# Two MLP products by seven block products each, beside each other, in an attention and MLP kernel

## The chip, the cores and the metric

The kernel runs on one core of one Trainium2 chip. The core has TensorE (PE in the profile; its weight loads are PEld), VectorE (DVE), ScalarE (ACT), GpSimd (POOL) and SyncE (SP), which work at the same time and wait for each other through semaphores; each takes its own instructions in order. 16 DMA engines move data between HBM and the on-chip memory SBUF. TensorE writes its results to PSUM, which has eight banks of 128 partitions x 512 fp32 numbers. The metric is the time of one execution in microseconds, the median of several runs; lower is better.

## The reference, cut to what matters

There are 4 sequences of 768 positions and 8 heads of width 64. Attention with decay, block by block (the reference uses blocks of 64; the kernel uses blocks of 128, which gives the same sums):

```python
intra = np.einsum('bhic,bhjc->bhij', qb, kb) * Dmask[None]      # lam ** (i - j) for i >= j
intra = np.einsum('bhij,bhjd->bhid', intra, vb)
inter = np.einsum('bhid,bhde->bhie', qb * lam_pow[None], kv_state)
out[:, :, sl] = intra + inter
kv_state = lam_block * kv_state + np.einsum('bhsd,bhse->bhde', kb * rev_pow, vb)
...
x = attn_out.transpose(0, 2, 1, 3).reshape(B * S, H * D)         # 3072 x 512
h = x @ w_in                                                     # 512 x 2048
g = 0.5 * h * (1.0 + erf(h / sqrt(2)))
return g @ w_out                                                 # 2048 x 512
```

## The kernel before

The 24 chunks (4 sequences of 6 chunks of 128 positions) are taken in order of the sequence: chunk n belongs to sequence n // 6. Four chunks in a row form a group of 512 rows; there are six groups. The MLP of group g and the attention of group g+1 are issued together, so that TensorE alternates between them.

The MLP of a group is a list of blocks (`mlp_blocks`, line 276). The first product has 16 blocks (`mm1`, line 281): four matmuls of 128 x 128 x 512 into one PSUM bank, then ScalarE's Gelu writes 512 columns of g in bf16 (line 290). The second product goes by 128 rows (`mm2`, line 295): 16 matmuls of 512 columns into a bank in four parts, then ScalarE copies the bank to SBUF (line 305) and SP stores it (line 306). The last 128 rows of the last group go in two halves of 256 columns (`mm2_half`, line 309, matmuls on line 315).

The attention of a chunk has these steps. POOL issues the loads of k, q and v (`load`, line 63), which turn fp32 into bf16 and read rows of 64 numbers. Each load waits until the POOL load eight places before it has landed. For the first two groups k and q are transposed by TensorE (line 174), from chunk 8 on by DMA from SP's queue (`dma_transposes`, line 185), after POOL has multiplied q by its decay (line 190). POOL multiplies k by its decay too (line 167). `scores` (line 193) makes eight small matmuls and DVE masks them (line 202). `next_state_full` (line 234) makes four matmuls, and DVE adds the old state (line 245) and multiplies by the decay (line 246). `outputs` (line 249) makes four matmuls with the state and eight with v, and ACT or DVE copies the result to the x of the MLP.

The order for TensorE is written out by hand for groups 0 and 1 (lines 371 to 397 and `group0`, line 425), and from chunk 8 on it is by due times, as shares of a group's work (`todo`, line 438). In the first microseconds TensorE also runs matmuls on zeros (`keep_warm`). The weights are loaded behind group 0's q, k, v, and group 1's loads stand behind the weights in POOL's queue.

## Time and profile before

| | |
|---|---|
| median of 3 runs | 218.49 us (217.81 to 218.74) |
| span of the profiled execution, first to last instruction (its own time isn't given apart) | 217.5 us |
| TensorE busy | 204.9 us, 94% of the span |
| VectorE busy | 74.8 us, 34% |
| ScalarE busy | 91.1 us, 42% |
| GpSimd busy | 105.8 us, 49% |
| mean granted TensorE clock | 0.997 |
| DMA | 24.35 MB in 100272 packets, 92960 of them under 512 B |

The profile is one execution. An instruction's row gives its start, its length, the engine, the line of the kernel, what it writes and reads, and in square brackets how long its engine was idle before it and what ended that. Matmuls overlap one another: a row's mean length is longer than the distance at which they follow, and the chain, which gives the time of a run of matmuls, shows that distance. A table by stretches gives busy time of each engine in each stretch. Groups give a line's instructions together: count, busy time, mean ns of one, and the idle time before them.

### The profile page before, as it was taken

To read this page: it belongs to the slowest core of one execution; us is meant where nothing else is said; L and a number is where in the kernel's file an instruction comes from. 1 tells how busy PE (TensorE), PEld (TensorE's weight loads), DVE (VectorE), ACT (ScalarE), POOL (GpSimd) and SP (SyncE) were. 2 spreads that over 40 slices of the span, in tenths; PEclk is the share of its full clock that TensorE was granted. 3 is DMA by queue.
4 is the path that set the end of the run, shared out by engine and by line. 5 is a ranking of instruction groups with operands and counts; after the bars stand their busy time and mean duration, and the time that the engine had idled before them with its cause. 6 is when DMAs were issued, how large, how long until landed. Compare 5 with 4: busy or idle time off the path is not lost.

```text
span 217.5 us, 3545 instructions
## 1 busy us (share of the span) xinstructions
PE 204.9 (94%) x1422; PEld 102.9 (47%) x1446; DVE 74.8 (34%) x120; ACT 91.1 (42%) x169; POOL 105.8 (49%) x120
## 2 busy tenths in 40 slices
PE   7679999999987999999999999999999999999993
PEld 2355444555443544444545444544445545444452
DVE  5884000478516243316225323315415323100000
ACT  6975772434563321365221375221465221566121
POOL 8998333998999999276950809113000000000000
PEclk9999999999999999999999999999999999999998
DMA  5999999999999999999999497515251012100112
GB/s 37 149 169 203 198 194 183 156 208 148 177 150 126 164 128 138 215 110 104 109 114 160 77 180 62 37 48 146 74 98 24 3 57 88 50 0 3 48 49 96
DMA packets 100272, 24.35 MB, mean 112 GB/s; under 512 B 92960, under 2 KB 97312, under 8 KB 100256
## 3 DMA queue, kind: packets, MB, share of 16 engines
q0 software_dynamic: 79104, 13.64, 84.4%
q1 hardware_dynamic: 21152, 10.50, 22.7%
q8 instruction: 11, 0.18, 0.3%
q14 instruction: 5, 0.04, 0.1%
HBM read 27.27 MB, written 6.29 MB: 154 GB/s over the span
## 4 chain that ended last, share of the span: by engine, by line
PE 73%; DMA 14%; POOL 9%; issue 2%; ACT 0%; POOLq 0%
PE o_ps L300 33%; PE h_ps L288 28%; DMA q_t<-in_q_dram 8%; DMA qT<-q_hat 3%; DMA w_in_t<-in_moe_w_in_dram 3%; PE o_ps L263 3%; PE sc_ps L198 3%; POOL k_t L65 3%; POOL q_t L65 2%; POOL v_t L65 2%; PE kv_ps L238 2%; PE o_ps L315 2%; PE o_ps L253 2%; POOL k_dec L167 1%; POOL q_hat L190 1%
## 5 line engine op out<-in xcount | busy, mean ns | idle before, releaser
L288 PE MATMUL h_ps<-x_t,w_in_t 128*128 128x512 bf16 (+2 forms) x378 | 84.8, 377 | 1.0 <-DMA w_in_t<-in_moe_w_in_dram 0.5
L300 PE MATMUL o_ps<-w_out_t,g_t 128*128 128x512 bf16 x355 | 81.8, 379 | 0.8 <-issue 0.3
L290 ACT ACTIVATE g_t<-h_ps 128x512 bf16<-128x512 f32 x96 | 57.3, 597 | 35.3 <-PE h_ps L288 35.3
L288 PEld LDWEIGHTS <-w_in_t 128*128 128x128 bf16 x388 | 37.3, 98 | 43.8 <-DMA w_in_t<-in_moe_w_in_dram 0.6
L300 PEld LDWEIGHTS <-g_t 128*128 128x128 bf16 x368 | 34.7, 98 | 39.6
L305 ACT COPY o_sb<-o_ps 128x512 f32<-128x512 f32 x23 | 13.5, 586 | 68.3 <-PE o_ps L300 62.5
L202 DVE TENSOR_TENSOR sc_m<-sc_ps,dmask 128x512 bf16<-128x512 f32 x48 | 30.8, 683 | 16.1 <-PE sc_ps L198 15.8
L273 DVE CAST x_t<-o_ps 128x512 bf16<-128x512 f32 x16 | 11.1, 692 | 71.4 <-PE o_ps L263 71.4
L190 POOL TENSOR_TENSOR q_hat<-q_t,lam_p 128x512 bf16<-128x512 bf16 x16 | 16.9, 1056 | 20.0 <-DMA qT<-q_hat 19.0
L167 POOL TENSOR_TENSOR k_dec<-k_t,lam_m 128x512 bf16<-128x512 bf16 x16 | 17.7, 1106 | 14.0 <-PE kv_ps L238 8.1
L65 POOL DMA_DIRECT2D k_t<-in_k_dram x24 | 22.1, 920 | 4.0 <-DMA w_out_t<-in_moe_w_out_dram 2.1
L65 POOL DMA_DIRECT2D q_t<-in_q_dram x24 | 21.5, 897 | 4.2 <-DMA w_out_t<-in_moe_w_out_dram 3.4
L65 POOL DMA_DIRECT2D v_t<-in_v_dram x24 | 21.4, 894 | 3.4 <-DMA w_out_t<-in_moe_w_out_dram 1.7
L198 PE MATMUL sc_ps<-qT,kT 64*128 64x128 bf16 x192 | 9.5, 218 | 3.8 <-DMA qT<-q_hat 2.6
L246 DVE TENSOR_TENSOR state<-tmp,lam_blk 128x512 bf16<-128x512 f32 x13 | 12.1, 932 | 0.5
L183 DVE TENSOR_TENSOR qT<-t_ps,lam_q 128x512 bf16<-128x512 bf16 x8 | 5.5, 689 | 18.9 <-PE t_ps L174 18.7
L263 PE MATMUL o_ps<-sc_m,v_t 128*64 128x128 bf16 x192 | 10.1, 225 | 0.0
L198 PEld LDWEIGHTS <-kT 64*128 64x128 bf16 x192 | 5.7, 94 | 8.3 <-issue 4.7
L361 PE MATMUL idle_ps<-idle 128*128 128x512 bf16 x21 | 7.5, 473 | 1.2 <-DVE idle L94 1.2
L245 DVE TENSOR_TENSOR tmp<-kv_ps,state 128x512 f32<-128x512 f32 x12 | 8.2, 681 | 0.0
L180 ACT COPY kT<-t_ps 128x512 bf16<-128x512 bf16 x7 | 4.1, 579 | 9.4 <-PE t_ps L174 9.4
L263 PEld LDWEIGHTS <-v_t 128*64 128x64 bf16 x192 | 6.2, 109 | 3.3 <-issue 0.8
(57 smaller groups left out, 82.7 us busy)
## 6 DMA issues: line engine op xcount, KB each, us to landing
out_dram<-o_sb SPq DMA_DIRECT2D x23, 256.0 KB, 2.6
k_t<-in_k_dram POOLq DMA_DIRECT2D x24, 128.0 KB, 4.6
q_t<-in_q_dram POOLq DMA_DIRECT2D x24, 128.0 KB, 5.9
v_t<-in_v_dram POOLq DMA_DIRECT2D x24, 128.0 KB, 5.9
w_in_t<-in_moe_w_in_dram POOLq DMA_DIRECT2D x4, 512.0 KB, 7.9
w_out_t<-in_moe_w_out_dram POOLq DMA_DIRECT2D x4, 512.0 KB, 15.1
kT<-k_t SPq DMA_TRANSPOSE x16, 4.7
qT<-q_hat SPq DMA_TRANSPOSE x16, 4.0
```

Source lines behind the costliest of these rows:

```text
L65: nc.gpsimd.dma_start(raw[n, name], chunk_of(name, n))
L167: eng.tensor_mul(c.k_dec, c.k, scale[:, :, None].to_broadcast((128, H, D)))
L190: nc.gpsimd.tensor_mul(q_hat, c.q, lam_p[:, :, None].to_broadcast((128, H, D)))
L198: nc.tensor.matmul(sc_ps[hi][:, hp, :], c.kT[p, hp, :], c.qT[p, hp, :], start=True, stop=True)
L202: nc.vector.tensor_mul(c.sc_m[:, :, hi, :], sc_ps[hi], dmask_r[:, :, hi, :])
L246: nc.vector.tensor_mul(new, tmp, lam_blk)
L263: nc.tensor.matmul(o_ps[hi * D:(hi + 1) * D, hp, :], c.v[:, 2 * hp + hi, :], c.sc_m[:, hp, hi, :], start=(c.sb == 0 and hp == 0), stop=Tru ...
L273: nc.vector.tensor_copy(c.x_o, c.o_ps)
L288: nc.tensor.matmul(h_ps[:, lo:hi], w_in_t[:, ki, kf * 128:(kf + 1) * 128], x_t[:, ki, lo:hi], start=(ki == 0 and lo == 0), stop=(ki == NK1 ...
L290: nc.scalar.activation(g_t[:, kf, :], h_ps, ACT.Gelu)
L300: nc.tensor.matmul(om[io], g_t[:, kf, io * C:(io + 1) * C], w_out_t[:, kf, :], start=(kf == 0), stop=(kf == NK2 - 1))
L305: nc.scalar.copy(o_sb, om[io])
```

## The change

The rows of a group now come from all four sequences: group g is chunk g of each, so that there are six groups of 512 rows as before, and the attention of a group needs the states of four sequences after chunk g-1. x and g are laid out by sequence.

Both MLP products are cut into 2 x 2 blocks and computed by seven block products with sums of blocks before and after (Winograd's form of Strassen's scheme): the first product for groups 2 to 5, the second for groups 1 to 5. The sums of the weights (`s_in`, `t_out`) are made once; those of x (`sums_x`, four a group) and of g (`sums_g`, 16 a group) in bf16 by DVE. In a unit of the first product (`unit_slots`, four units a group, each for 4 of the 16 blocks of 128 hidden columns) ACT copies P5 to SBUF and P1 from one PSUM bank into the other, the next block products add on top of what is there, and DVE forms Z and W; four Gelus of 512 columns read the results. In the second product (`mm2_slots`) ACT copies P1, P5 and the last block, and DVE makes four sums; the stores are of 256 columns of two sequences. All of these matmuls have 256 columns.

From group 2 on, the order of a period is a string: `a` is four matmuls of a unit of group g's first product, `m` four matmuls of group g-1's second product, `v` a visit of the attention of group g+1, `x` a sum of x. `later(n, ...)` issues DVE's work n slots behind. The first product of groups 0 and 1 and the second of group 0 stay plain, with strings for their order (`PHASE1`, `PHASE2`).

The attention changes too. v is scaled by POOL (`scale_v`, one operation for two sequences) in place of k and the mask's decay; q's decay is multiplied in when DVE empties the outputs (`lam_q`), so q is transposed as loaded, and POOL's product on q is gone. Loads, scalings and DMA transposes (`crossbar`) are of two sequences each. In groups 0 and 1 the tiles are packed with two sequences of 64 partitions, two positions a partition, so that rows of 128 numbers are read. DVE adds the old state, POOL multiplies by the decay.

```diff
-    def load(n, name):
-        raw[n, name] = qkv_pool.tile([128, H, D], BF16, tag=name, name=f"{name}_t")
-        nc.gpsimd.dma_start(raw[n, name], chunk_of(name, n))
+    PACKED = (0, 1)
+    def load(g, pair, name):
+        if g in PACKED:
+            t = raw_pool.tile([128, H, 2, D], BF16, tag="r" + name, name="raw_" + name, bufs=3 if name == "v" else 4)
+            for b in range(2):
+                G.dma_start(t[b * 64:(b + 1) * 64].rearrange("p h t d -> p h (t d)"),
+                            dram[name][2 * pair + b, :, g * C:(g + 1) * C, :].rearrange("h (p t) d -> p h (t d)", t=2))
+        else:
+            t = raw_pool.tile([128, 2, H, D], BF16, tag="r" + name, name="raw_" + name, bufs=3 if name == "v" else 4)
+            G.dma_start(t.rearrange("p b h d -> p (b h) d"),
+                        dram[name][2 * pair:2 * pair + 2, :, g * C:(g + 1) * C, :].rearrange("b h si d -> si (b h) d"))
+        raw[g, pair, name] = t
...
+    s_in = [w_pool.tile([128, 2, d_ff // 2], BF16, name=f"s_in{i}") for i in range(4)]
+    t_out = [None if i == 2 else w_pool.tile([128, NK2 // 2, d_model // 2], BF16, name=f"t_out{i}") for i in range(4)]
+    t_out[2] = w_out_t[:, 0:NK2 // 2, d_model // 2:]
...
-    def decay_k(c, eng):
...
-    def dma_transposes(c):
-        c.kT = work_pool.tile([128, HP, C], BF16, tag="kT", name="kT")
-        c.qT = work_pool.tile([128, HP, C], BF16, tag="qT", name="qT")
-        q_hat = work_pool.tile([128, H, D], BF16, tag="qh", name="q_hat")
-        nc.sync.dma_start_transpose(out=c.kT, in_=c.k.rearrange("p h d -> p (h d)"))
-        nc.gpsimd.tensor_mul(q_hat, c.q, lam_p[:, :, None].to_broadcast((128, H, D)))
-        nc.sync.dma_start_transpose(out=c.qT, in_=q_hat.rearrange("p h d -> p (h d)"))
+    def scale_v(g, pair, eng):
+        if g in PACKED:
+            vs[g, pair] = work.tile([128, H, 2, D], BF16, tag="vs", name="vs", bufs=3)
+            eng.tensor_mul(vs[g, pair], raw[g, pair, "v"], lam_mp_b)
+        else:
+            vs[g, pair] = work.tile([128, 2, H, D], BF16, tag="vs", name="vs", bufs=3)
+            eng.tensor_mul(vs[g, pair], raw[g, pair, "v"], lam_m_b2)
+    def crossbar(g, pair):
+        for d, n in ((kT, "k"), (qT, "q")):
+            d[g, pair] = work.tile([128, 2, HP, C], BF16, tag=n + "T", name=n + "T", bufs=3)
+            SY.dma_start_transpose(out=d[g, pair].rearrange("p b h c -> p (b h) c"),
+                                   in_=raw[g, pair, n].rearrange("p b h d -> p (b h d)"))
...
+    def scores(g, s, tags, lags):
+        pair, i = divmod(s, 2)
+        sc = [bank(t, [128, HP, C]) for t in tags]
+        for hp in range(HP):
+            for hi in range(2):
+                p = slice(hi * D, (hi + 1) * D)
+                P.matmul(sc[hi][:, hp, :], kT[g, pair][p, i, hp, :], qT[g, pair][p, i, hp, :], start=True, stop=True)
+        def mask(hi):
+            V.tensor_mul(sc_m[g, s][:, :, hi, :], sc[hi], cm_b)
+            done.add(("m", g, s, hi))
+        for hi in range(2):
+            later(lags[hi], lambda hi=hi: mask(hi))
+    def outputs(g, s, tag, lag):
+        need(("m", g, s, 0), ("m", g, s, 1), ("st", g, s // 2))
+        pair, i = divmod(s, 2)
+        o = bank(tag, [128, HP, C])
+        for hp in range(HP):
+            for hi in range(2):
+                p = slice(hi * D, (hi + 1) * D)
+                P.matmul(o[p, hp, :], states[g][p, s, hp, :], qT[g, pair][p, i, hp, :],
+                         start=(hp == 0), stop=False, skip_group_check=True)
+        for hp in range(HP):
+            for hi in range(2):
+                P.matmul(o[hi * D:(hi + 1) * D, hp, :], vs[g, pair][:, i, 2 * hp + hi, :], sc_m[g, s][:, hp, hi, :],
+                         start=False, stop=True, skip_group_check=True)
+        def empty():
+            V.tensor_mul(xs[g][:, :, s, :], o, lam_q)
+            done.add(("x", g, s))
+        later(lag, empty)
+    def state_products(g, pair, tag, lag):
+        kv = bank(tag, [128, 2, HP, D])
+        for i in range(2):
...
+        def add():
+            tmp = work.tile([128, 2, HP, D], F32, tag="tmp", name="tmp", bufs=1)
+            V.tensor_add(tmp, kv, states[g][:, 2 * pair:2 * pair + 2])
+            G.tensor_mul(states[g + 1][:, 2 * pair:2 * pair + 2], tmp, lam_c_b)
+            done.add(("st", g + 1, pair))
+        later(lag, add)
...
+    def sums_w_in(a, b):
+        lo, hi = slice(a * 128, b * 128), slice(1024 + a * 128, 1024 + b * 128)
+        w = slice(a * 128, b * 128)
+        s1, s2, s3, s4 = (s[:, :, w] for s in s_in)
+        V.tensor_add(s1, w_in_t[:, 0:2, hi], w_in_t[:, 2:4, hi])
+        V.tensor_sub(s2, s1, w_in_t[:, 0:2, lo])
+        V.tensor_sub(s3, w_in_t[:, 0:2, lo], w_in_t[:, 0:2, hi])
+        V.tensor_sub(s4, w_in_t[:, 2:4, lo], s2)
+    def sums_g(g, u, i, eng=V):
+        t = gts[g]
+        lo, hi = slice(2 * u, 2 * u + 2), slice(8 + 2 * u, 10 + 2 * u)
+        gLL, gLH, gHL, gHH = t[:, lo, 0:256], t[:, lo, 256:512], t[:, hi, 0:256], t[:, hi, 256:512]
+        s1, s2, s3, s4 = (s[:, lo, :] for s in gs[g])
+        if i == 1:
+            need(("g", g, u, "Z"), ("g", g, u, "W"))
+            eng.tensor_add(s1, gLH, gHH)
+        elif i == 2:
...
-        blocks = [(mm1(kf), 4 * T) for kf in range(NK2)]
-        if g == 0:
-            blocks += [(mm2(io, part), 4 * 512) for pair in range(0, M, 2) for part in range(parts)
-                       for io in (pair, pair + 1)]
-        else:
-            last = g == NG - 1
-            blocks += [(mm2(io, part), 4 * 512) for io in range(M - last) for part in range(parts)]
-            if last:
-                blocks += [(mm2_half(M - 1, half), 16 * 256) for half in range(2)]
+        def prod(dst, w, f0, x_of, start):
+            for b in range(2):
+                for ko in range(2):
+                    P.matmul(dst[:, b, :], w(ko, f0 + b * 128), x_of(ko),
+                             start=(start and b == 0 and ko == 0), stop=True, skip_group_check=True)
...
+        def seed():
+            if "V" in st and "Y" in st:
+                A.copy(st["V"], st["Y"])
+                done.add(("seed", g, u))
+        def p5():
+            need(("tx", g, 1))
+            st["V"] = bank("uV", [128, 2, 256])
+            prod(st["V"], ws(1), lo, tx(1), True)
+            st["Vs"] = work.tile([128, 2, 256], F32, tag="Vs", name="Vs")
+            A.copy(st["Vs"], st["V"])
+            seed()
+        def p1():
+            need(("x", g, 0), ("x", g, 1))
+            st["Y"] = bank("uY", [128, 2, 256])
+            prod(st["Y"], wl, lo, x11, True)
+            seed()
+        def p2():
+            need(("seed", g, u))
+            prod(st["V"], wh, lo, x21, False)
+            gelu("X", t[:, bl, 0:256], st["V"])
+        def p6():
+            need(("seed", g, u), ("tx", g, 2))
+            prod(st["Y"], ws(2), lo, tx(2), False)
+            def z():
+                st["Z"] = bank("uZ", [128, 2, 256])
+                V.tensor_add(st["Z"], st["Y"], st["Vs"])
+                done.add(("Z", g, u))
+            later(lags["Z"], z)
+        def p7():
+            need(("Z", g, u), ("tx", g, 3))
+            prod(st["Y"], ws(3), lo, tx(3), False)
+            def w():
+                V.tensor_add(st["Vs"], st["Y"], st["Vs"])
+                done.add(("W", g, u))
+                gelu("W", t[:, bh, 256:512], st["Vs"])
+            later(lags["W"], w)
+        def p3():
+            need(("Z", g, u))
+            prod(st["Z"], ws(4), lo, x22, False)
+            gelu("Z", t[:, bl, 256:512], st["Z"])
+        def p4():
+            need(("W", g, u), ("tx", g, 4))
+            prod(st["Y"], wh, hi, tx(4), False)
+            gelu("Y", t[:, bh, 0:256], st["Y"])
+        return [p5, p1, p6, p2, p7, p3, p4]
...
+        def add(key, dst, src, other, th=None, dh=None):
+            def go():
+                st[dst] = o_tile() if th is not None else f32(dst)
+                V.tensor_add(st[dst], st[src], st[other])
+                done.add((key, g))
+                if th is not None:
+                    store(st[dst], th, dh)
+            return go
+        def after(n):
+            if n == 1:
+                st["P1s"] = f32("P1s")
+                A.copy(st["P1s"], st["Y"])
+            elif n == 5:
+                st["Vs"] = f32("Vs")
+                A.copy(st["Vs"], st["R"])
+            elif n == 6:
+                later(lags["M"][0], add("Zs", "Zs", "Y", "Vs"))
+            elif n == 2:
+                later(lags["M"][1], add("C11", "o11", "R", "P1s", 0, 0))
+            elif n == 7:
+                later(lags["M"][2], add("C22", "o22", "Y", "Vs", 1, 1))
+            elif n == 3:
+                later(lags["M"][3], add("C12", "o12", "R", "Zs", 0, 1))
+            elif n == 4:
+                o = o_tile()
+                A.copy(o, st["Y"])
+                store(o, 1, 0)
+        plan = [(1, "Y", aLL, b11, ()), (5, "R", sg(1), to(1), (("gs", 1),)), (6, "Y", sg(2), to(2), (("gs", 2),)),
+                (2, "R", aHL, b21, ()), (7, "Y", sg(3), to(3), (("gs", 3), "Zs")),
+                (3, "R", sg(4), b22, (("gs", 4), "C11")), (4, "Y", aHH, to(4), ("C22",))]
+        slots = []
+        for n, dst, a, b, needs in plan:
+            new = dst == "R" or n == 1
+            for u in range(4):
+                def run(n=n, dst=dst, a=a, b=b, u=u, new=new, needs=needs):
+                    for x in needs:
+                        need((x, g) if isinstance(x, str) else (x[0], g, u, x[1]))
+                    if u == 0 and new:
+                        st[dst] = bank("m" + dst, [128, 2, 256])
+                    for io in range(2):
+                        for kf in (2 * u, 2 * u + 1):
+                            P.matmul(st[dst][:, io, :], a(kf, io), b(kf),
+                                     start=(new and u == 0 and io == 0 and kf == 0), stop=True, skip_group_check=True)
+                    if u == 3:
+                        after(n)
+                slots.append(run)
+        return slots
...
+    V.memset(state_1, 0.0)
+    keep_warm(11, True)
+    p_transposes(0, 0, "k", "mY", (A, A))
+    keep_warm(3)
...
+    scale_v(0, 0, G)
+    load_w_in(2, 4)
+    load_w_in(4, 8)
...
+    scale_v(0, 1, G)
+    load_w_in(8, 12)
+    load_w_in(12, 16)
+    for a in (0, 4, 8, 12):
+        load_w_out(a, a + 4)
...
+    PHASE1 = "k p w w q p w p p s s w p p p k p o p q p s s p p p o p c c p p"
...
+    def visit(g, i, lags):
+        if i > 0:
+            outputs(g, i - 1, "a2", lags[0])
+        if i < B:
+            scores(g, i, ab, lags[1:3])
+        if i == 2 and g + 1 < NG:
+            crossbar(g + 1, 0)
+            crossbar(g + 1, 1)
+        if i == B and g + 1 < NG:
+            state_products(g, 0, "a0", lags[1])
+            state_products(g, 1, "a1", lags[2])
...
+    PHASE2 = "t z n p p t p v t p p p p v p p p t v p p v p p v p x x x p x"
...
+    PERIOD = "amammmaavmamvamaamvammammaamamaamavmmammvaamammaamamamaamamaxmxxx"
+    LZ = "0200"
+    LW = "0110"
+    LS = "1222222212202222"
+    LM = "0000"
+    LV = "000000001000000"
+    for g in range(2, NG):
+        new_g(g)
+        m2 = mm2_slots(g - 1, dict(M=digits(LM, 0, 4)))
+        new_gs(g)
+        att = g + 1 < NG
+        if att:
+            new_x(g + 1)
+            scale_v(g + 1, 0, G)
+            scale_v(g + 1, 1, G)
+            next_loads(g + 2)
...
+        for u in range(4):
+            sl = dict(zip("5162734", unit_slots(g, u, dict(Z=int(LZ[u]), W=int(LW[u]), S=digits(LS, u, 4)))))
+            a += [sl[c] for c in ("1562734" if u == 0 else "5162734")]
+        visits = list(range(5))
+        sums = [3, 1, 2, 4]
+        for c in seqs:
+            if c == "a":
+                a.pop(0)()
+                tick()
+            elif c == "m":
+                m2.pop(0)()
+                tick()
+            elif c == "v":
+                i = visits.pop(0)
+                if att:
+                    visit(g + 1, i, digits(LV, i, 3))
+            elif c == "x":
+                i = sums.pop(0)
+                if att:
+                    sums_x(g + 1, i)
+        assert not (a or m2 or visits or sums)
+        flush()
+    for s in mm2_slots(NG - 1, dict(M=(0, 0, 0, 0))):
+        s()
+        tick()
```

691 lines of the change are left out of this document (380 added, 311 removed).

## The prediction

> **What bounds the kernel now.** I read the page's busy table and slices first, to find the engine that is never idle; then a table of busy time by stretches; then the chain that ended last, for the price of a run of products; then groups and single instructions for the other engines' prices.
>
> ```profile
> span 217.5 us, 3545 instructions
> PE 204.9 (94%) x1422; PEld 102.9 (47%) x1446; DVE 74.8 (34%) x120; ACT 91.1 (42%) x169; POOL 105.8 (49%) x120
> PE   7679999999987999999999999999999999999993
> ```
> ```profile
> 20.00:33.50 13.50, 13.45 (x73) 6.31 (x72) 0.84 (x2) 9.41 (x18) 5.32 (x7) 1.00 1.23 198
> 105.00:137.00 32.00, 31.79 (x216) 15.73 (x218) 11.51 (x18) 11.74 (x20) 17.23 (x19) 1.00 1.14 118
> 200.00:214.00 14.00, 13.95 (x80) 7.74 (x79) 0.00 (x0) 2.73 (x5) 0.00 (x0) 1.00 0.18 65
> 214.00:217.50 3.50, 0.02 (x1) 0.00 (x0) 0.00 (x0) 0.37 (x1) 0.00 (x0) 0.80 0.11 38
> ```
>
> The columns of the second view are the stretch, then busy time of PE, PEld, DVE, ACT and POOL, the granted clock, the DMA share and GB/s. From 20 us to 214 us TensorE works without a gap at clock 1.00, and in a middle stretch of 32 us the others are busy for 11.5 to 17.2 us. So the end is set by TensorE's work, plus about 20 us of start and a tail of 3.5 us. The profile gives its span, 217.5 us; the median of the runs shown is 218.49, 1.0 us above, and I add that 1.0 to a sum of spans. About 0.5% (1.1 us) is what a measurement can tell from no change.
>
> Prices on TensorE, from the chain (start, length, what):
>
> ```profile
> 43.04 0.22 PE kv_ps L238 x4
> 104.80 1.73 PE o_ps L300 x8
> 106.75 0.34 PE o_ps L263 x8
> 107.10 0.33 PE sc_ps L198 x8
> 210.53 3.51 PE o_ps L315 x32
> ```
> ```profile
> 16.06 0.41 PE L259 MATMUL o_ps<-qT,state 64*64 64x128 bf16 x8 [0.55 <-ACT x_t L271]
> 16.40 0.41 PE L263 MATMUL o_ps<-sc_m,v_t 128*64 128x128 bf16 x8
> 20.35 0.32 PE L213 MATMUL kv_ps<-v_t,k_dec 128*64 128x64 bf16 x8
> 20.59 1.47 PE L288 MATMUL h_ps<-x_t,w_in_t 128*128 128x512 bf16 x6
> ```
>
> A product of 512 columns costs 1.73/8 = 0.216 us, one of 256 columns 3.51/32 = 0.110, of 128 columns 0.22/4 = 0.055; half-size tiles of 128 columns cost (16.40-16.06)/8 = 0.0425, those of 64 columns (20.59-20.35)/8 = 0.030. The 256-column row matters most: each of its 32 products loads its own weights, as all new products do, and it costs half of a 512-column one. The shorter products hold their pace.
>
> **The change, part by part.** Seven products of half-size blocks replace eight. A plain product of a group is 64 x 0.216 = 13.8 us; seven block products are 7 x 16 x 0.110 = 12.3 us. It is done for the first product of groups 2 to 5 and the second of groups 1 to 5: nine times 1.5 = 13.7 us less on TensorE, where nothing covers it, so all of it counts unless something else becomes late.
>
> Span of the new kernel, stage by stage:
>
> Start. Loads of groups 0 and 1 become two DMAs of 64 partitions each, with half as many rows twice as long.
>
> ```profile
> 1.38 1.06 POOL k_t L65
> ```
> ```profile
> 16.86 0.59 ACT L271 CAST x_t<-o_ps 128x512 bf16<-128x512 f32 x1 [0.85 <-PE o_ps L263]
> 17.02 3.03 POOL L91 DMA_DIRECT2D w_out_t<-in_moe_w_out_dram  x4
> 19.37 0.88 PEld L288 LDWEIGHTS <-w_in_t 128*128 128x128 bf16 x8 [0.63 <-DMA w_in_t<-in_moe_w_in_dram]
> 21.66 0.88 POOL L65 DMA_DIRECT2D q_t<-in_q_dram  x1 [0.72 <-DMA w_in_t<-in_moe_w_in_dram]
> 37.49 0.88 POOL L65 DMA_DIRECT2D q_t<-in_q_dram  x1 [1.62 <-DMA w_out_t<-in_moe_w_out_dram]
> ```
> ```profile
> L190 POOL TENSOR_TENSOR q_hat<-q_t,lam_p 128x512 bf16<-128x512 bf16 x16 | 16.9, 1056 | 20.0 <-DMA qT<-q_hat 19.0
> L273 DVE CAST x_t<-o_ps 128x512 bf16<-128x512 f32 x16 | 11.1, 692 | 71.4 <-PE o_ps L263 71.4
> ```
>
> POOL issues 13 DMAs at about 0.8 us (4 took 3.03) from 0.9 (the first starts at 1.38 now, behind two iotas that move behind it) to 11.3; the scaling of v is twice the 1.056 us row, 2.1, to 13.4; two weight DMAs and the second scaling end at 17.1; then 32 small products (1.4) and two copies with decay (2 x 0.69) give group 0's last x at 19.9. Two half products and 14 whole blocks of 0.864 (0.9 + 12.1) and 32 state products (0.96) end at 33.8. Now this point is near 33.5, so the start is worth nothing either way.
>
> Group 1's keys. The order of the new code transposes k of group 1 before anything else of the second product. In the rows, a POOL load released by a weight DMA at 21.66 and one at 37.49 lie six weight DMAs apart: 2.64 us each. In the new order six of that size remain when POOL leaves the second scaling (17.1, plus 0.8 to issue), so the last weight lands at 33.7; half a transfer more (1.3) brings the keys at 35.0: a wait of 1.2 us with nothing to cover it. It is 0 if DMA runs ahead, 5.0 if the weights end at 37.5 as now; I take 1.2.
>
> Second product of group 0 beside group 1's attention: 16 x 0.864 = 13.8; four transposes of 16 tiles (4 x 0.68 = 2.7); four halves of scores (2.7); two outputs of 8 whole and 32 half-size products (3.6): 22.8.
>
> First product of group 1 beside group 2's attention: 13.8; state products of group 1 0.96; four sequences with scores 0.33, state 0.34, values 0.34 (4.0); new state 32 x 0.030 = 0.96: 19.8. DVE gets 16 sums of g here and about 22 operations on PSUM, POOL four sums of w_out and four more tensor operations, so DVE is nearly as full as TensorE. I add 1.0 (0 to 3).
>
> Periods g = 2, 3, 4: 56 slots x 4 x 0.110 = 24.6, attention 5.0, together 29.6, where now such a group takes 32.4:
>
> ```profile
> 137.22 1.73 PE o_ps L300 x8
> 169.64 1.73 PE o_ps L300 x8
> ```
>
> The period of group 5, without attention, is 24.6, the last second product 28 x 4 x 0.110 = 12.3. The tail: the last block is copied whole (0.59 where half took 0.37) and stored in twice the size: 3.5 + 0.7 = 4.2.
>
> What the other engines must do in a full period:
>
> ```profile
> L290 ACT ACTIVATE g_t<-h_ps 128x512 bf16<-128x512 f32 x96 | 57.3, 597 | 35.3 <-PE h_ps L288 35.3
> L305 ACT COPY o_sb<-o_ps 128x512 f32<-128x512 f32 x23 | 13.5, 586 | 68.3 <-PE o_ps L300 62.5
> L202 DVE TENSOR_TENSOR sc_m<-sc_ps,dmask 128x512 bf16<-128x512 f32 x48 | 30.8, 683 | 16.1 <-PE sc_ps L198 15.8
> L315 PE MATMUL o_ps<-w_out_t,g_t 128*128 128x256 bf16 x32 | 3.7, 273 | 0.0
> L245 DVE TENSOR_TENSOR tmp<-kv_ps,state 128x512 f32<-128x512 f32 x12 | 8.2, 681 | 0.0
> L182 DVE COPY kT<-t_ps 128x512 bf16<-128x512 bf16 x1 | 0.4, 416 | 0.0
> L65 POOL DMA_DIRECT2D k_t<-in_k_dram x24 | 22.1, 920 | 4.0 <-DMA w_out_t<-in_moe_w_out_dram 2.1
> ```
>
> ACT: 16 Gelus x 0.597, 8 copies that seed the chains and 3 of the second product x 0.586: 16.0 of 29.6. Covered. POOL: two scalings (4.2), two state products (2.1), six loads of double size (0.92 to 1.84 each, 5.5 to 11): 12 to 17, covered. SP has four double transposes for eight single ones, with stores behind them; its waits for loads issued a third of a period earlier are covered.
>
> DVE: 8 masks, 4 outputs, 2 state sums, 8 sums inside the units (Z, W), 4 of the second product, 26 with a PSUM operand x 0.683 = 17.8; and 20 sums of 512 bf16 elements whose operands all lie in SBUF (16 of g, 4 of x). No row shows these. The ends are 0.416 (the only row with 16-bit data on both sides, one input) and 0.69 (two fp32 inputs, below); I take 0.42, since the data is 16-bit throughout: 8.4. Together 26.2 of 29.6, where it was 11.5 in 32. That is 89% on a queue in strict order, so it must cost something. [...]
>
> Following one period slot by slot with these prices, the chain of a unit (P1, seed, P6, Z, P7, W, P4, Gelu) is four slots of four products, each with the 0.16 us by which a product outlasts its pace (0.273 against 0.110), 0.6 each; two ACT operations of 0.6 and two DVE sums of 0.7: 5.0 us in a unit of 29.6/4 = 7.4, and mostly fits. Three places don't. In the fifth visit the two state sums share one tmp buffer, so DVE waits for POOL's 1.05 us product between them, and W of unit 2 behind it comes 0.45 us late. At the turn of the period the sums of x for the next group come out 0.35 after P5 wants them. P1 of unit 2 waits 0.15 for a Gelu. I take 1.0 in each full period (0 to 5), and 0.5 in group 5's, where the unit has 6.1 us.
>
> Sum: 33.8 + 1.2 + 22.8 + 19.8 + 1.0 + 3 x (29.6 + 1.0) + 24.6 + 0.5 + 12.3 + 4.2 = 212.0 us of span; with the 1.0 around it 213.0.
>
> **The rivals.**
>
> *Two queues want one port (slower).* DVE's sums with two SBUF inputs stop while POOL reads.
>
> ```profile
> L246 DVE TENSOR_TENSOR state<-tmp,lam_blk x13: 691/693/1834, 44.4 to 174.5; 128x512 bf16<-128x512 f32 x13
> ```
> ```profile
> 58.66 1.54 DVE L246 TENSOR_TENSOR state<-tmp,lam_blk 128x512 bf16<-128x512 f32 x1
> 58.55 1.09 POOL L190 TENSOR_TENSOR q_hat<-q_t,lam_p 128x512 bf16<-128x512 bf16 x1
> 59.56 1.54 POOL L167 TENSOR_TENSOR k_dec<-k_t,lam_m 128x512 bf16<-128x512 bf16 x1
> ```
>
> The only DVE line of the steady part with two SBUF inputs takes 0.69 us, but 1.54 beside a POOL product, which ended first; the next POOL product then took 1.54 for 1.05. In the new kernel the two scalings of v, 2.1 us each, follow the state products on POOL, at 24 to 29 us of the period, and the sums of unit 2's g are issued there, with Z of unit 3 behind them in DVE's queue. If each scaling stops one sum, Z3 ends near 31.4, where P7 of unit 3, at 27 us of products in the order and 1.2 of stalls before it, wants it at 28.2: 3.2 us a period, 9.6 in three, 222.6 us. Against it: sums may slip between, and the wait needs the overlap at that place. It decides from 1.9 us a period (218.5 - 213.0 = 5.5 over three). [...]
>
> *Sums at 0.69.* Twenty sums cost 0.27 more: DVE has 31.6 us in a period, and 1.1 of waiting for tmp, 32.7 against 30.6: 3 x 2.1, and 2 beside group 1's first product: 221.3. Against it stands the 0.416 row.
>
> *Everything is hidden.* No keys late, no stalls: 212.0 - 1.2 - 1.0 - 3.0 - 0.5 = 206.3, with 1.0: 207.3. For it: ACT at 54%, and long slack in most units.
>
> *Keys late by 5.0.* 216.8.
>
> *The change doesn't do what it says:* short products too slow to gain. The 32 products in 3.51 us speak against it; I give it no chance of its own.
>
> **How the numbers follow.** Forecast, a mostly hidden schedule, 213.0: 0.45, with 209.5 to 217 as its own range (stalls of 0 to 2 us a period). All hidden 0.20; the port 0.20; sums at 0.69 0.08; keys 0.07. Faster by over 0.5% (under 217.4): 0.20 + 0.44 + 0.06 = 0.70. Within 0.5%: what lies between, the port at half its price (217.8) and the upper edge of the keys: 0.10. Slower: 0.20. The range 207 to 222 leaves out under 2 in 10.
>
> **What would show it.** Right: in a period of groups 2 to 4 TensorE's products start 30 to 31.5 us apart, DVE is busy about 26 us, sums of g take near 0.42. Wrong: periods of 33 us with sums of g at 1 to 2.5 us beside the scaling of v (the port); sums all near 0.69; PE idle for more than 2 us before group 1's k transposes. A total under 208 would say that the three stalls I found by walking the slots aren't there; one over 222 that a wait I haven't seen (SP's stores behind transposes, say) holds TensorE.

## The result and the profile after

The changed kernel takes 244.16 us (median of 4 runs, 243.49 to 244.71) where the kernel before took 218.15 beside it (216.87 to 218.74): a ratio of 1.120, 95% interval 1.116 to 1.125. It is 26 us slower; the forecast was 213.0, with 207 to 222 as its range. The profiled execution took 243.9 us, with a span of 242.1, 30.1 above the forecast's 212.0. Some executions of one kernel take a few per cent longer than its others; the ratios leave those out, the medians don't, and a kernel given below without a ratio has one time only.

The page of the changed kernel: busy times, slices (tenths in 40 slices), and the chain that ended last.

```profile
span 242.1 us, 5321 instructions
PE 205.8 (85%) x2242; PEld 146.6 (61%) x2256; DVE 163.4 (68%) x278; ACT 95.9 (40%) x173; POOL 88.1 (36%) x87
...
PE   7698984927989869399986999985999999999893
...
DVE  4454721799649999966976696886897855666231
...
POOL 8987235980117974970089200080000000000000
PEclk9999996797999999779997999999999999999999
...
PE 54%; DVE 18%; DMA 9%; POOL 7%; issue 5%; ACT 4%; DVEq 0%; POOLq 0%; ACTq 0%
```

TensorE, busy for 190 of the 194 us from 20 to 214 us before, now has holes up to slice 28 and none after it. DVE's busy time is up from 74.8 to 163.4 us and DVE holds 18% of the chain. The granted clock falls in four places. POOL's slices end where the holes end.

The same by stretches (columns: stretch, busy time of PE, PEld, DVE, ACT, POOL, granted clock, DMA share, GB/s). The rows are the second product of group 0, the first product of group 1, then the periods of groups 2, 3 and 4:

```profile
39.40:69.00 29.60, 23.32 (x267) 12.30 (x272) 21.60 (x32) 5.07 (x9) 14.30 (x13) 0.85 1.45 139
69.00:92.80 23.80, 20.14 (x254) 10.33 (x258) 21.55 (x30) 9.54 (x16) 17.10 (x14) 1.00 1.16 92
92.80:134.90 42.10, 34.41 (x354) 26.63 (x353) 33.13 (x51) 15.32 (x28) 25.45 (x20) 0.88 1.42 120
134.90:169.10 34.20, 30.56 (x353) 24.96 (x353) 26.26 (x45) 14.95 (x28) 5.97 (x4) 1.00 0.87 92
169.10:199.20 30.10, 29.58 (x320) 24.28 (x320) 23.17 (x45) 14.91 (x28) 0.00 (x0) 1.00 0.11 36
```

Three periods with nearly the same work on TensorE take 42.1, 34.2 and 30.1 us. They differ in POOL's busy time: 25.5, 6.0 and nothing, and also in what the DMA engines move (120, 92 and 36 GB/s); the experiments have to tell the two apart. ACT copies P1 of the second product once a period, which gives a mark for all later comparisons:

```profile
95.60 0.59 ACT L560 COPY P1s<-p_mY 128x512 f32<-128x512 f32 x1
...
137.71 0.59 ACT L560 COPY P1s<-p_mY 128x512 f32<-128x512 f32 x1
...
171.87 0.58 ACT L560 COPY P1s<-p_mY 128x512 f32<-128x512 f32 x1
...
202.06 0.59 ACT L560 COPY P1s<-p_mY 128x512 f32<-128x512 f32 x1
```

What POOL does there is the scaling of v (timeline of POOL):

```profile
48.25 4.02 POOL L175 TENSOR_TENSOR vs<-raw_v,lam_mp 128x1024 bf16<-128x1024 bf16 x2
...
74.88 3.94 POOL L178 TENSOR_TENSOR vs<-raw_v,lam_m 128x1024 bf16<-128x1024 bf16 x2
...
96.49 4.12 POOL L178 TENSOR_TENSOR vs<-raw_v,lam_m 128x1024 bf16<-128x1024 bf16 x2
...
123.87 3.94 POOL L178 TENSOR_TENSOR vs<-raw_v,lam_m 128x1024 bf16<-128x1024 bf16 x2
...
159.63 3.94 POOL L178 TENSOR_TENSOR vs<-raw_v,lam_m 128x1024 bf16<-128x1024 bf16 x2
```

Two pairs fall into the period of group 2 (92.8 to 134.9), one into that of group 3, none into that of group 4. Beside them stand DVE's sums of 512 bf16 elements (timeline of DVE):

```profile
44.28 0.41 DVE L357 TENSOR_TENSOR t_out<-w_out_t 128x512 bf16<-128x512 bf16 x1
44.73 2.12 DVE L358 TENSOR_TENSOR t_out<-w_out_t,t_out 128x512 bf16<-128x512 bf16 x1
46.88 3.64 DVE L359 TENSOR_TENSOR t_out<-w_out_t,t_out 128x512 bf16<-128x512 bf16 x1
50.45 2.12 DVE L346 TENSOR_TENSOR s_in<-w_in_t 128x512 bf16<-128x512 bf16 x1
52.60 0.43 DVE L347 TENSOR_TENSOR s_in<-s_in,w_in_t 128x512 bf16<-128x512 bf16 x1
...
96.84 2.00 DVE L401 TENSOR_TENSOR gs<-g_t,gs 128x512 bf16<-128x512 bf16 x1
98.77 2.12 DVE L404 TENSOR_TENSOR g_t<-g_t 128x512 bf16<-128x512 bf16 x1
100.81 0.69 DVE L494 TENSOR_TENSOR p_uZ<-p_uY,Vs 128x512 f32<-128x512 f32 x1
```
```profile
101.55 1.01 PE L444 MATMUL p_uY<-tx,s_in 128*128 128x256 bf16 x4 [2.52 <-DVE p_uZ L494]
```

A free sum takes 0.41 to 0.43 us. Beside a scaling it takes 1.5 to 2.1, waiting for the POOL instruction of 2 us under way; Z of the unit stands behind two such sums in DVE's queue, and TensorE behind Z. 17 of the 124 sums take more than 0.5 us, and over 0.42 us each the sums take 22.9 us in all. Of this 16.6 us fall on ten sums beside the ten scalings (the one of 3.64 us met two DMA issues first), 3.9 us on four sums beside nothing of POOL's but DMA issues (the one at 44.73 among them), and 2.2 us on three beside POOL's state products and sums. PE's waits over the run:

```profile
PE p_uY L444 <- DVE p_uZ L494: 7.2, 3, 2.5
PE t_ps L247 <- DVE sc_m L272: 5.5, 1, 5.5
PE t_ps L247 <- DMA raw_k<-in_k_dram: 4.4, 2, 3.9
```

### The profile page after: what moved, and what is told of

Read it like the earlier page. It is cut to its first block, busy times and chain, and to the rows that moved or that the text cites. A ratio compares the mean times of both kernels' runs of the same rounds, so it can differ in the third digit from the quotient of the medians.

```text
span 242.1 us, 5321 instructions
## 1 busy us (share of the span) xinstructions
PE 205.8 (85%) x2242; PEld 146.6 (61%) x2256; DVE 163.4 (68%) x278; ACT 95.9 (40%) x173; POOL 88.1 (36%) x87
## 4 chain that ended last, share of the span: by engine, by line
PE 54%; DVE 18%; DMA 9%; POOL 7%; issue 5%; ACT 4%; DVEq 0%; POOLq 0%; ACTq 0%
PE p_mY L591 12%; PE p_uY L444 11%; PE p_mR L591 9%; DMA raw_k<-in_k_dram 7%; PE p_uV L444 5%; ACT g_t L456 3%; DVE g_t L404 3%; DVE gs L395 3%; PE p_uZ L444 2%; DMA raw_v<-in_v_dram 2%; PE p_uY L425 2%; DVE gs L398 2%; PE p_a L212 2%; PE p_a L208 2%; PE p_a L192 2%
## 5 line engine op out<-in xcount | busy, mean ns | idle before, releaser
L444 PEld LDWEIGHTS <-s_in 128*128 128x128 bf16 x256 | 25.1, 99 | 14.5 <-issue 10.2
L444 PE MATMUL p_uY<-tx,s_in 128*128 128x256 bf16 x128 | 20.0, 280 | 8.3 <-DVE p_uZ L494 7.2
L591 PEld LDWEIGHTS <-gs 128*128 128x128 bf16 x240 | 23.6, 99 | 3.4
L395 DVE TENSOR_TENSOR gs<-g_t 128x512 bf16<-128x512 bf16 x20 | 13.2, 662 | 13.7 <-ACT g_t L456 13.7
L591 PE MATMUL p_mY<-w_out_t,g_t 128*128 128x256 bf16 x160 | 21.1, 272 | 0.7 <-ACT o_q L574 0.7
L196 DVE TENSOR_TENSOR sc_m<-p_a,cmask 128x512 bf16<-128x512 f32 x32 | 20.5, 680 | 0.0
L178 POOL TENSOR_TENSOR vs<-raw_v,lam_m 128x1024 bf16<-128x1024 bf16 x8 | 15.9, 2013 | 0.0
L404 DVE TENSOR_TENSOR g_t<-g_t 128x512 bf16<-128x512 bf16 x20 | 13.2, 662 | 0.1
L591 PE MATMUL p_mY<-t_out,g_t 128*128 128x256 bf16 x80 | 12.4, 286 | 0.0
L591 PE MATMUL p_mR<-t_out,gs 128*128 128x256 bf16 x80 | 12.2, 283 | 0.0
## 6 DMA issues: line engine op xcount, KB each, us to landing
w_out_t<-in_moe_w_out_dram POOLq DMA_DIRECT2D x4, 512.0 KB, 14.6
```

Source lines behind the costliest of these rows:

```text
L178: eng.tensor_mul(vs[g, pair], raw[g, pair, "v"], lam_m_b2)
L196: V.tensor_mul(sc_m[g, s][:, :, hi, :], sc[hi], cm_b)
L395: eng.tensor_add(s1, gLH, gHH)
L404: eng.tensor_sub(s3, gLL, gLH)
L444: P.matmul(dst[:, b, :], w(ko, f0 + b * 128), x_of(ko), start=(start and b == 0 and ko == 0), stop=True, skip_group_check=True)
L591: P.matmul(st[dst][:, io, :], a(kf, io), b(kf), start=(new and u == 0 and io == 0 and kf == 0), stop=True, skip_group_check=True)
```

## The experiments

All stages in one table, in us: the forecast's terms, the changed kernel, and four of the kernels below. A period runs from mark to mark (the copy of P1, 2.8 us after the start of a period and 2.4 after that of the last product, so the forecast's 25.1 for group 5 stands as 24.7 and its end as 14.1).

| stage | forecast | changed | v filled | quarters | all placed, v on POOL | all placed, v on ACT |
|---|---|---|---|---|---|---|
| to group 1's key transposes | 35.0 | 39.4 | 38.8 | 39.7 | 35.4 | 35.4 |
| second product of group 0 | 22.8 | 29.6 | 20.9 | 27.7 | 28.4 | 22.1 |
| first product of group 1 | 20.8 | 23.8 | 21.7 | 20.6 | 22.3 | 20.3 |
| to the first mark | 2.8 | 2.8 | 2.8 | 4.7 | 2.8 | 3.4 |
| period of group 2 | 30.6 | 42.1 | 32.8 | 38.4 | 41.2 | 32.1 |
| period of group 3 | 30.6 | 34.2 | 31.8 | 32.8 | 35.2 | 31.5 |
| period of group 4 | 30.6 | 30.2 | 30.2 | 30.2 | 30.2 | 29.8 |
| period of group 5 | 24.7 | 25.4 | 25.4 | 25.4 | 25.5 | 25.5 |
| last product, tail | 14.1 | 14.6 | 14.6 | 14.6 | 14.6 | 14.6 |
| span | 212.0 | 242.1 | 219.0 | 234.1 | 235.5 | 214.7 |

### First: the reads, the keys, the clock, the products

The kernel before took 219.71 beside these four, 218.53 beside the run with zeros in the periods.

**POOL writes v without reading.**

```diff
...
-            eng.tensor_mul(vs[g, pair], raw[g, pair, "v"], lam_m_b2)
+            eng.memset(vs[g, pair], 0.5)
```

> From group 1 on POOL fills the scaled v with a constant in place of multiplying v by its decay, so POOL writes as much but reads nothing (this part of the computation is left out). Theory 1, the port: VectorE's sums with two SBUF inputs are held for 22.9 us in all, most of it beside the scalings of v (2.0 us each); without these reads the sums of g take 0.42 us again, the stalls at 51 to 55, 97 to 101, 124 to 130 and 160 to 165 us go, and with them the halved clock that follows: 10 to 18 us less, 226 to 234. Theory 2, the long chain of each unit (product, copy, product, sum, product, sum, product, Gelu) is what holds TensorE: the time changes by less than 3 us. Theory 3, any occupation of VectorE's port by POOL counts, fills too: the sums stay at 1 to 2 us beside the fills.

Measured: 220.8 us. The gain of 23 is above the range given: held sums fall from 22.9 to 4.5 us, the granted clock is 0.999 over the run, and the fill also waits for no load, which matters below. That POOL's scaling costs the time is shown; by which way, not yet.

**Group 1's keys early.**

```diff
-    for a in (0, 4, 8, 12):
-        load_w_out(a, a + 4)
...
+    load_w_out(0, 4)
+    load(1, 0, "k")
+    load_w_out(4, 8)
+    load(1, 0, "q")
+    load_w_out(8, 12)
+    load_w_out(12, 16)
+    load(1, 0, "v")
...
```

> Only the order of loads changes: k and q of group 1's first two sequences are issued before the second and third quarter of w_out. Theory: TensorE stands 4.1 us for the keys and then works for 6.8 us at half clock; with the keys there at 35 us both go, worth 4 to 7 us, 237 to 240. Rival: the second product of group 0 is held by the next thing anyway (the masks behind VectorE's sums at 46 to 54 us), and the end moves by less than 1.5 us.

Measured: 243.54 us, no gain beyond the changed kernel's own 243.49 to 244.71. The 3.9 us wait is gone, but the next steps wait longer: the second product of group 0 takes 31.1 us for 29.6 and the first product of group 1 25.4 for 23.8 (the waits for Z are now 8.7 us for 7.2, and 2.3 us are for POOL's scaled v).

**Zeros ahead of the keys.**

```diff
+    keep_warm(18, True, "a2")
     script(PHASE1, attn_1)
```

> 18 matmuls on zeros (3.9 us at full clock) stand in front of the first transposes of group 1, so that TensorE works while it would wait for the keys; the keys come no sooner. If the wait costs mainly by the halved clock behind it, the clock stays at 1.00 from 38 to 45 us, the products there run twice as fast, and up to 3 us are gained (239 to 242). If only the wait itself counts, or VectorE sets the pace after it, the time is the same within 1 us.

Measured: 242.51 us, 1.7 less, between the two expectations. The clock stays at 1.00 up to 50 us and the second product of group 0 takes 26.8 us for 29.6; 1.4 us of that is lost again in the first product of group 1, where a halved stretch now begins at 84 us.

**Zeros in the waits of the periods.**

```diff
+                if g < 4 and len(a) in (24, 3):
+                    keep_warm(8, True, "a2")
                 a.pop(0)()
```

> The changed kernel with eight matmuls on zeros put ahead of the seventh block product of two units in the periods of groups 2 and 3, where TensorE waits longest; the port conflict is kept. If the halved clock after those waits costs by itself, the clock stays at 1.00 near 99 to 107 us and 130 to 134 us and the time falls by 2 to 5 us to 239 to 242. If the halved stretches only lie where TensorE waits for DVE anyway: 243 to 245, and periods of 42 and 34 us as before.

Measured: 244.71 us. By stretches, the first product of group 1 and the periods of groups 2 and 3 in this kernel:

```profile
69.30:95.70 26.40, 22.61 (x253) 11.38 (x257) 21.87 (x30) 9.54 (x16) 17.33 (x14) 0.87 1.17 102
95.70:133.90 38.20, 34.08 (x368) 26.54 (x369) 32.04 (x49) 15.12 (x28) 23.83 (x19) 1.00 1.33 112
133.90:169.80 35.90, 33.88 (x367) 26.50 (x369) 27.04 (x47) 14.91 (x28) 7.37 (x6) 1.00 0.91 94
```

The period of group 2 runs at 1.00 and is 4 us shorter, so the halved clock is worth about that much there. The total doesn't fall: a halved stretch came earlier (0.87 in the first row), and the zeros cost 1.7 in the period of group 3, where the clock had been full. The clock adds to the loss; it is not its root.

**Plain products in the new order**, no sums, loads and attention as changed.

```diff
...
-    for u in range(4):
-        later(2 * u, lambda u=u: sums_w_in(2 * u, 2 * u + 2))
...
-        m2 = mm2_slots(g - 1, dict(M=digits(LM, 0, 4)))
...
+        for i in range(16):
+            mm1_plain(g, i, tags[i % 3])
...
+            mm2_plain(g - 1, i // 4, i % 4, ("mY", "mR")[(i // 4) % 2])
...
```

> Groups across sequences, loads, scalings and the attention as in the changed kernel, but all MLP products are plain and none of the sums of blocks is made. TensorE has 13.7 us more to do than with block products. Theory 1 (sums held at the port, then the clock): with VectorE at half its load nothing holds TensorE but the keys, a period takes 64 x 2 x 0.216 + 5.0 = 32.7 us, and the whole about 35.3 + 4.1 + 22.8 + 19.8 + 3 x 32.7 + 27.7 + 13.8 + 4 = 225.6, faster than with block products. If the new order of the attention and loads were the cause, it would stay above 240.

Measured: 233.81 us. It has none of the sums, so none to hold, and is still 14 us above the kernel before. TensorE waits 5.1 us for the DMA transposes of q and 3.4 for the keys, POOL 4.7 for raw v. So the new grouping and its loads cost time by themselves (a period here alternates the two products by a plain loop, not by the change's string); with v filled, the block products end 13 us earlier than these plain ones. Plain products with v out of the way weren't run.

### Second: another engine for v

The kernel before took 218.53 beside the first of the three runs on DVE and both on ACT, 218.18 beside the other two on DVE.

**v scaled by DVE**, at the same place, then later.

```diff
     def scale_v(g, pair, eng):
+        if g > 0:
+            eng = V
```

> The changed kernel with the scaling of v of groups 1 to 5 done by DVE instead of POOL; everything is still computed, and DVE gets about 2 us more of work in a period, in which it was busy for under 27 us without stalls. If POOL's reads of v hold DVE's sums (theory), periods fall from 42.1 and 34.2 us to about 32 to 33, and the time to 218 to 224 us, near the 220.8 of the run that filled v instead. If the 23 us of that run came from what it left out of the arithmetic or from DMA of raw v being no longer waited for (rival), the time stays above 235, since DVE now has more to do and all data are waited for.

Measured: 239.4 us, a miss. DVE takes 1.23 us for what POOL takes 2.0, but stands in order behind the load:

```profile
42.20 1.23 DVE L177 TENSOR_TENSOR vs<-raw_v,lam_mp 128x1024 bf16<-128x1024 bf16 x1 [13.88 <-DMA raw_v<-in_v_dram]
46.55 1.23 DVE L177 TENSOR_TENSOR vs<-raw_v,lam_mp 128x1024 bf16<-128x1024 bf16 x1 [3.12 <-DMA raw_v<-in_v_dram]
```

**The same, issued later.** The call moves from the head of a period to the fifth visit before it, and for group 1 into the second product of group 0:

```diff
...
             state_products(g, 1, "a1", lags[2])
+            scale_v(g + 1, 0, V)
+            scale_v(g + 1, 1, V)
...
```

> The scaling of v on DVE as in the run that took 239.4, but issued behind the last transposes' wait in the second product of group 0 and, for later groups, in the fifth visit, when raw v has long landed. If that run was slow because DVE stood 17 us behind the loads of v and then did the scaling at the head of each period (theory): 219 to 226. If DVE's own amount of work is the bound (rival): 235 to 240.

Measured: 239.3 us, a miss again. DVE's long waits for loads are gone, but TensorE waits for DVE in other places: 5.6 us for W's sums, 3.6 for the scaled v, 1.9 for a sum of x. With the placements of the next sections added (keys early, the state sum's last addition later, the third sums of w_out on DVE):

> The run before with the keys early, the state sum's last addition three slots later and the third sum of w_out on DVE. DVE then has 28 to 29 us of work in a period of 30, so I expect it behind the quarters: 217 to 223. Under 216 would say that DVE's amount isn't what the periods wait for; over 225 that it is.

Measured: 233.06 us, ratio 1.064 (1.056 to 1.072). Here one scaling waited 4.6 us for raw v, and a sum of x behind it kept TensorE 6.4 us. Which part of the loss is DVE's amount of work and which the loads wasn't taken apart.

**v scaled by ACT**, as 8 or 16 small scaled copies spread over the slots.

```diff
...
+                v_list.append((g, pair, lambda h=h: A.activation(
+                    vs[g, pair][:, :, h, :], raw[g, pair, "v"][:, :, h, :], ACT.Copy, scale=lam_m[:, h:h + 1])))
...
```

> The scaling of v of groups 1 to 5 done by ACT in 8 or 16 small scaled copies a sequence pair, spread over the slots. ACT is busy for 16 us of a period of 30, so 2 to 4 us more there fit. Theory (POOL's reads hold DVE's sums): 217 to 222 us, below the DVE version. Rival (DVE's plain amount of work is the bound, and the reads only move its waits): no gain over 240, or no difference to the DVE version.

Measured: 231.49 us: 12.7 less than changed, but between the two expectations. Held sums are down to 4.1 us; the keys' wait of 4.4 us stays, and TensorE waits 7.4 us for ACT's seeds and Gelus.

**With the keys early and the state sum's last addition later.**

```diff
...
-    LV = "000000001000000"
+    LV = "000000001000003"
```

> As the run before, with group 1's first keys and queries loaded between the parts of w_out, and the second state sum's last addition three slots later. With the port conflict gone, the keys' wait of 4.1 us should now be worth time, since nothing else holds the place: 212 to 217 us, faster than the kernel before. If DVE still holds the place that the keys left, as in the run that moved the keys alone: 217 to 221, no gain over the run before.

Measured: 222.54 us, ratio 1.016 (1.005 to 1.028). That is outside both expectations, but the two edits are worth 9.0 us here, 4.5 of it before group 1's transposes, where the keys alone gained nothing clear while POOL held the sums.

### Third: POOL in smaller pieces, and POOL's queue

The kernel before took 218.18 beside the first two, 217.89 beside the others.

**Quarters** (n is 2 of the 8 heads from group 1 on).

```diff
...
-            eng.tensor_mul(vs[g, pair], raw[g, pair, "v"], lam_m_b2)
+            for h in range(0, H, n):
+                w = slice(h, h + n)
+                eng.tensor_mul(vs[g, pair][:, :, w], raw[g, pair, "v"][:, :, w], lam_m_b2[:, :, w])
```

> The changed kernel with each scaling of v on POOL cut into four instructions of a quarter (256 elements a partition) from group 1 on; the same bytes are read by the same engine. If a sum of DVE waits only for the POOL instruction that is under way (theory), no sum beside the scaling takes longer than about 1.0 us (0.42 + 0.5) where it took 2.0, and the time falls to 222 to 234 us. If a sum waits until POOL has no more reads to do (rival), the sums beside it still take 2 to 4 us and the time stays within 240 to 247.

Measured: 235.83 us, 8.3 less than changed and 1.8 above the range, while the sums do what the theory says (DVE, then POOL, in this kernel):

```profile
121.69 0.72 DVE L409 TENSOR_TENSOR g_t<-g_t 128x512 bf16<-128x512 bf16 x1
122.33 0.83 DVE L403 TENSOR_TENSOR gs<-gs,g_t 128x512 bf16<-128x512 bf16 x1
```
```profile
120.19 5.33 POOL L183 TENSOR_TENSOR vs<-raw_v,lam_m 128x256 bf16<-128x256 bf16 x8
```

0.72 and 0.83 us where they took 2.0, beside POOL instructions of 5.33/8 = 0.67 us: these sums were held for no longer than the one POOL instruction under way. Held sums are 12.1 us. Since engine, reads and order of POOL's queue are the same, this run shows that the hold itself costs time. Yet the period of group 2 keeps 38.4, with a wait of 4.2 us for transposed queries that had been hidden behind the held sums.

**Quarters, keys early, state sum later, third sums of w_out on DVE.**

```diff
...
-        "t": [lambda i=i: sums_w_out(2 * i, 2 * i + 2, (3,), G) for i in range(4)],
+        "t": [lambda i=i: sums_w_out(2 * i, 2 * i + 2, (3,)) for i in range(4)],
```

> The quarters of the run before, and three more edits: group 1's first keys and queries loaded between the parts of w_out, the last addition of the second state sum three slots later, and the third sum of w_out on DVE instead of POOL. By the stages of the earlier runs (36.0 to the second product, 22.2 beside group 1's attention, 21 to 22 for the first product of group 1, periods of 32 to 33, 32, 30 and 26, 12.4 and 4.1 at the end) 216 to 220 us if the quarters free the sums; 230 to 240 if they don't.

Measured: 228.19 us, ratio 1.045 (1.037 to 1.052): between the two expectations. It waits 3.7 us for the transposed queries, 2.5 for v.

**Loads ahead of the scalings in POOL's queue**, in the changed kernel, then with the quarters and the rest. `scale_after_loads` issues five loads, the two scalings, then the last load.

```diff
-            scale_v(g + 1, 0, G)
-            scale_v(g + 1, 1, G)
-            next_loads(g + 2)
+            scale_after_loads(g + 1)
...
```

> The changed kernel with one move: in POOL's queue five of the six loads of the next group stand ahead of the scalings of v, not behind them. If the order on POOL costs by itself (theory), the DMA engines have no hole near 73 to 85 us and the time falls by 4 to 10 us, to 234 to 240; the sums are still held for 2 us each. If the loads' lateness is hidden behind the held sums: 242 to 246.

> The quarters, the early keys, the later addition of the state sum, the third sum of w_out on DVE (228.2 together), and the loads ahead of the scalings. If the loads were late behind the scalings, the waits of 3.7 us for the transposed queries and 2.5 us for the scaled v go, and the half clock after them (1.7): 218 to 222. If not: 226 to 230.

Measured: 248.62 us, 4.5 more than changed, and 235.60 us, ratio 1.080 (1.075 to 1.086), 7.4 more than without the move. Both lie above all that was expected, and the theory fell. In the first kernel the DMA engines move more from 73 to 85 us (107 GB/s for 42), as the theory has it, but less later (20 GB/s for 160 from 92 to 99 us); and with the queries in time v is late, since five issues of 1.18 us stand ahead of it (the waits of the second kernel):

```profile
PE p_a L217 <- POOL vs L183: 9.1, 8, 4.2
```

Either order makes something late. POOL issues six loads (7.1 us) and scales (4 us) in one queue, and both are wanted soon.

### Fourth: the best placing, with v on ACT and on POOL

The kernel before took 217.89, 217.82 (two kernels) and 217.88 us beside these.

**ACT's copies spread** over one slot in two, from the fourth visit on.

```diff
...
-        v_some(v_rate[0])
...
+        v_some(v_rate[0] if v_rate[0] >= 1 else slot_no[0] % 2)
...
```

> The version with the scaling on ACT (222.5) with the third sum of w_out on DVE and ACT's scaled copies one in two slots from the fourth visit on, so that fewer seeds and Gelus stand behind them. PHASE2 falls from 23.4 to 21 to 22.5 us, periods of groups 2 and 3 from 34.5 to 32 to 34: 216 to 220 us, about the kernel before. Above 221: the copies on ACT are not what the periods wait for.

Measured: 220.09 us, ratio 1.005 (1.001 to 1.008).

**Group 3's queries before the state products of group 1, its v first behind them.**

```diff
...
+        "h": lambda: (load(3, 0, "q"), load(3, 1, "q")),
...
```

> The version with spread copies on ACT (220.1 median), with group 3's queries loaded before the state products of group 1 and its v first behind them. If the 3.1 us wait in the period of group 2 is raw v's arrival, it goes, with the halved clock behind it: 214 to 217 us, faster than the kernel before by 0.5 to 2%. If the DMA engines are full and only the order changes: 218 to 221.

Measured: 219.55 us, ratio 1.007 (1.004 to 1.010): as its rival expected, and by the ratios no gain. The longest wait of a seed is 1.2 us, behind a lump of scaled copies on ACT, and the clock stays at 1.00 from 36 to 204 us; the wait of 3.1 us before it was read in an execution of 222.9 us, above that kernel's median, so what its end is worth isn't shown.

**The same placing, v on POOL as in the change.**

> The same placing of keys, queries, state sum and sums of w_out, with the scaling of v by POOL in whole instructions as in the change. If the held sums and the loads behind the scalings are what the change lost (theory): 230 to 240 us, 14 to 24 over the run before. If the placing of the loads was the main thing: 218 to 224.

Measured: 237.24 us. 17.7 us more than the run before: that is what the scaling on POOL costs, with the other loads, the state sum and the sums of w_out placed alike (the scalings stand at the head of a period again, and group 2's last v is loaded as in the change). The table, whose last column is the run below, shows where: the second product of group 0 and the periods of groups 2 and 3. PE waits 10.4 us for Z; held sums are 20.3 us against 4.2. How the 17.7 divides between the held sums, the order of POOL's queue and the halved clock wasn't taken apart.

**The last load of v behind the first visit**, so that no lump of copies is forced.

```diff
...
-                load(g, pair, n)
+                if (pair, n) != (1, "v"):
+                    load(g, pair, n)
...
+        if i == 1 and g + 1 < NG:
+            load(g + 1, 1, "v")
...
```

> The version with group 3's queries early (219.55), with the last load of v of each group issued behind the first visit, so that no lump of scaled copies stands ahead of the seeds at 63.6 and 83.2 us. If the lump is what those waits of 1.27 and 1.20 us are for: 216 to 218 us, level with the kernel before or up to 1% faster. If the copies only move and hold another seed: 218.5 to 220.5.

Measured: 217.42 us (12 runs) against 217.88, ratio 0.998 (0.9954 to 1.0005): the 26 us are won back, and the kernel is level with the one before, not shown faster. Its profiled execution, of 216.5 us, is the fastest of them; its stretches for the periods of groups 2, 3 and 4:

```profile
78.40:110.50 32.10, 30.45 (x352) 24.74 (x351) 27.30 (x51) 22.42 (x55) 16.94 (x15) 1.00 1.65 144
110.50:142.00 31.50, 30.30 (x352) 24.93 (x352) 25.12 (x47) 19.37 (x45) 2.50 (x3) 1.00 1.00 102
142.00:171.80 29.80, 29.23 (x317) 24.03 (x317) 22.36 (x43) 15.59 (x31) 0.00 (x0) 1.00 0.11 37
```

## Why the prediction was wrong

The forecast failed at the choice between two of its own cases. It took "1.0 in each full period (0 to 5)" from a walk over the slots in which every sum had its free price, and left the stop of DVE's sums by POOL's reads to a rival of 0.20, "against it: sums may slip between". They don't slip: each of the ten scalings of 2 us meets a sum. What came is the forecast's own sign of that rival, a period over 33 us with sums of 1 to 2.5 us beside the scaling of v.

By the table, the 30.1 us that the span is longer lie before group 1's keys (4.4), in the second product of group 0 (6.8), in the first product of group 1 (3.0), in the periods of groups 2 and 3 (11.5 and 3.6), and 0.8 in the rest.

**The rival was right in kind, and its size was off by its count.** Its 222.6 is 21.6 us short as well. It charged 3.2 us for each of three periods, with the scalings behind the state products. In the period of group 3 the excess is 3.6 (34.2 for 30.6), and group 4 has no scaling and 30.2 us. But POOL runs ahead of the order in which the periods are written: five pairs of scalings fall at 48, 75, 96, 124 and 160 us, the first two outside the periods and two in group 2's. There the excess is 11.5, of which about 4 is the halved clock by the run with zeros; the forecast has no term for a halved clock. Beside the scaling at 96.49 a sum takes 2.00 us for 0.42, and with POOL's reads of v left out held sums fall from 22.9 to 4.5 us; that a shared port is what holds them isn't shown.

**"22.8" for the second product of group 0 was a sum over TensorE alone**, and measured 29.6. DVE's sums of the weights stand there ahead of group 1's masks; three of them, of 2.12, 3.64 and 2.12 us, kept TensorE 5.5 us, the first beside DMA issues and not beside a scaling. With v on ACT and all placed the stage takes 22.1. "19.8 + 1.0" for group 1's first product measured 23.8, and 21.7 with v filled, 20.3 with v on ACT and all placed.

**Keys:** "1.2 (0 to 5.0)" was 3.9, in the range given. Moving them alone gained nothing clear, because the next thing was late as well.

**POOL's "12 to 17, covered"** named the amount, not the order. In POOL's queue the loads stand behind the scalings, which can wait for raw v (4.7 us in the kernel with plain products). That cost is seen only when the first is gone: 4.2 us for the queries with quarters.

**Right:** the sums at 0.42 (0.41 to 0.43 free), so the rival of 0.69 is out; the pace of the 256-column products, by the period of group 4, 30.2 for 30.6; group 5, 25.4 for 24.7; the end, 14.6 for 14.1. The version with everything placed has a span of 214.7 against 212.0, and a median time of 217.4 against 213.0, so the terms are near where no scaling holds a sum. But it took another engine for v, moved loads, a moved addition and a sum moved to DVE to get there, and its gain over the kernel before lies within the interval.

Why the start of "33.8" was 35.3 to 35.5 in all of these kernels wasn't taken apart.

## What to carry to other kernels

Before two-input sums are added to VectorE, list each GpSimd instruction that reads SBUF and each DMA that GpSimd issues, and price every one that can meet a sum at its full length (here a sum of 0.42 us took 1.5 to 2.1 beside a scaling of 2.0, and up to 2.12 beside DMA issues of 1.19), plus all that is queued behind the sum; don't count on gaps. A GpSimd product that costs little while VectorE makes few such sums can cost much when VectorE begins to sum: in the kernel before, 13 operations of VectorE with two SBUF inputs took 3.1 us in all over their free 0.69, and here the scaling on GpSimd cost 17.7 us with the other loads placed alike. Here the repair that won the time back was to move the scaling to ScalarE, in pieces, and then to move the loads; on VectorE itself it cost more (233.1 us at best). Read queues in their own order, not in the order of the stages in the code: work that waits for a load holds everything behind it, the next loads included (v's scaling held VectorE for 13.88 us, and GpSimd, with the loads behind it, for 4.7).
